# A decode block with its gradients: one kernel, the same instructions in another order

## The chip, the cores and the metric

The kernel runs on one core of one Trainium2 chip. The metric is device time in microseconds (us), from launch to end, as the median of several runs. The profile is one further execution; its span runs from the first to the last instruction on the core and leaves out what the device does before and after it.

## What is computed

The forward pass is a layer norm, a grouped attention over a cache and a gated bilinear layer, summed. The kernel returns that sum and the gradients with respect to all eight inputs that are differentiated.

```
xn = layernorm(x)                                   # x: 2 x 1 x 576
q  = (xn @ wq) -> 32 heads of 128                   # wq: 576 x 4096
p  = softmax(q . k_cache / sqrt(128))               # caches: 2 x 16 x 4096 x 128, two heads share one
A  = (p . v_cache) @ wo                             # wo: 4096 x 576
B  = ((xn @ w_gate) * (xn @ w_up)) @ w_down         # 576 x 4608, 4608 x 576
out = x + A + B
returned: out, and d(out . grad_out) / d(x, k_cache, v_cache, wq, wo, w_gate, w_up, w_down)
```

All inputs and outputs are bf16. There are only two rows of x, so nearly all the work is reading the caches and weights once and writing gradients of the same shapes once.

## The kernel before

**Tiling.** A cache head is one tile of 128 x 4096 (1 MiB), loaded by one DMA. The kernel walks 16 steps s; a step is one group of two cache heads for one of the two batch rows. Each step loads two heads of k and two of v (L1142), transposes them in 32 x 32 blocks on VectorE (DVE, L465), scores them on TensorE (PE, L1267), does the softmax in small operations on PE, DVE and ScalarE (ACT), contracts the probabilities and the score gradients with the caches (L1441), and forms the gradients of v and k as outer products (L1289). GpSimd (POOL) builds the block-diagonal operands of these outer products (L1255). Every step stores four tiles of 1 MiB: two heads of out_3 (gradient of v) and two of out_2 (gradient of k).

**Weights.** wq and wo come in eight slices, one per group (L1164, L1169); gate, up and down come in nine slices of 512 columns (L1184, L1191, L1197). Their gradients are also outer products (L726, L763, L825), stored as out_4 to out_8.

**Evictions.** An outer product is made in units. A unit fills a PSUM tile (three of them, `ps_o`) and is then copied as bf16 into a store tile, by ACT (L469) or DVE (L471). A 1 MiB store needs four units of 1024 columns. This copying and the block transposes are most of what ACT and DVE do. Below, a copy of 1024 columns is called a wide eviction.

**Order.** No engine's order is written by hand. Each piece of work is a generator (`turn`, `attend`, `dscores`, `outer`, `contract`, `fronts`, `backs`, `mlp`, `load_kv`, `load_ws` and so on). While the kernel is being built, the class `Order` (L88 to L262) runs all generators against assumed costs and decides which one goes next on each engine. Among the candidates of one engine that can start within `SLACK` of the earliest, the smallest priority goes first. A priority is `STEP * s + PR[name]`, with `HEAD` or `TAIL` added in the first two and last two steps, and a single offset from `OFF[name][s]`. An eviction goes to ACT or DVE by the earlier assumed end, with `BIAS` against DVE. `WQ_AT`, `WO_AT` and `MLP_AT` say after which cache load each weight slice is loaded. What comes out is a fixed program: one instruction list per engine, with semaphore waits.

**Queues.** All large DMAs, loads and stores alike, are issued by SyncE (SP) on one queue, 229 of them in order (here counted as row 1 to row 229). A row waits at SP for the store's evictions or for the load's free tile, and all rows behind it wait too. There are 16 tiles of 1 MiB for loads, transposes, store tiles and gate/up slices; at most 6 hold caches, 10 transposes, 5 stores and 2 gate/up slices. A DMA may be issued when the one eight before it has landed.

Of the kernel before, what the change touches and what calls it, by code (L numbers as in the profile page):

```python
# [104 lines left out]
class Order:  # L105

    HOP, TAIL, DRAIN = 0.07, 0.18, {"PE": 0.0, "ACT": 0.1, "DVE": 0.075, "POOL": 0.0}

# [86 lines left out]
    def run(self):  # L195
        while self.streams:
# [8 lines left out]
            if e is not None:  # L205
                t, _, s, e = min((c for c in cand if c[3] == e and c[0] <= t + SLACK[e]), key=lambda c: (c[1], c[0]))
            r = s.req
            value = None
            if r[0] in ("op", "any"):
                cost = r[2] if r[0] == "op" else next(c for x, c, _ in r[1] if x == e)  # L210
                quad = r[3] if len(r) > 3 else None
                if e == "PE":
                    end = t + cost + self.TAIL
                    if quad is not None and self.quad[:2] == (1 - quad, t):
                        cost, end = 0.02, max(t + self.TAIL, self.quad[2]) + 0.02
                    self.quad, self.kind = (quad, t + cost, end), r[6]
# [46 lines left out]
def EV(cols):  # L263
    return ("any", [("ACT", 0.16 + cols * 0.00083, 0.0), ("DVE", 0.145 + cols * 0.00104, cols / 1024 * BIAS)])

# [21 lines left out]
def PRIO(prio):  # L287
    return ("prio", prio)


def DMA(engine, cost, nbytes, row=8192):
# [3 lines left out]


NBIG, NWW, NBD = 16, 5, 3
CAP = {"kv": 6, "X": 10, "st": 5, "G": 2}
OFF = {"mload": {0: 271.6, 1: -102.6, 2: -55.0, 3: -1.2, 4: 302.0, 5: -37.8, 6: -3.1, 7: -261.9, 8: -10.9, 10: 33.1,
       11: 0.8, 12: -207.4, 13: 133.1, 14: -7.7, 15: 159.7}, "wload": {0: 133.7, 1: 303.1, 2: 22.2, 3: 90.3,  # L300
# [7 lines left out]
       11: 190.3, 12: -28.6, 13: -116.3, 14: -697.9, 15: 68.4}, "load": {0: 14.2, 1: -78.4, 2: 45.7, 3: 100.8,  # L308
       4: -197.6, 5: 28.3, 6: 554.3, 7: 177.4, 8: 2.5, 9: -143.0, 10: -2.3, 11: -21.3, 12: 8.4, 13: -73.3, 14: 100.6,
       15: -142.0}, "front": {0: -179.7, 1: 85.4, 2: -277.2, 3: -256.2, 4: 1826.5, 5: 49.9, 6: 24.7, 7: 68.7,  # L310
       8: 74.6, 9: -133.5, 10: 299.2, 12: -72.9, 14: -82.2}, "turn0": {0: -74.5, 1: 12.8, 2: -59.7, 4: -98.2,
       5: -13.7, 6: 27.8, 7: -195.0, 8: 25.3, 9: -324.6, 10: 62.5, 11: 150.3, 12: 36.5, 13: 374.6, 14: 6.0,
       15: 40.1}, "con": {0: -246.4, 1: 1581.7, 2: 912.6, 3: -19.4, 4: -192.0, 5: -376.3, 6: -83.8, 8: 66.8,
       9: -106.8, 10: 1369.4, 12: 147.6, 13: 65.7, 14: 198.1, 15: 79.0}, "W0": {0: 31.7, 1: -255.2, 2: 62.9,
       3: -322.1, 4: -90.7, 5: -152.2, 6: 579.2, 7: -124.9, 8: 27.6, 9: -89.0, 10: -18.9, 11: -62.1, 13: 324.8,
       14: 5.0, 15: 14.0}, "back": {0: -32.5, 1: 35.1, 2: -23.7, 3: -119.2, 4: 97.7, 5: 800.9, 6: -2327.5, 9: -276.5,
# [3 lines left out]
       9: -447.4, 10: 31.8, 11: -210.3, 12: -58.4, 13: -249.2, 14: -11.7, 15: 118.0}, "dsc": {0: -165.3, 2: -11.7,  # L320
       3: -436.2, 4: 52.6, 5: -31.9, 7: 88.0, 8: -832.8, 9: 9.9, 10: -27.9, 12: -325.8, 14: 576.3, 15: -5.7},
       "mlp": {0: 894.9, 1: 15.9, 3: -552.7, 4: -163.6, 5: -290.8, 6: 30.0, 7: -24.7, 9: -5.3, 10: -0.7, 11: -155.0,
       12: -3.1, 13: 1.8, 14: 185.9, 15: 66.1}, "att": {0: 223.1, 1: 245.8, 2: -323.8, 4: 2.7, 5: -249.3, 7: -26.2,
       8: -319.6, 9: -120.7, 10: -196.9, 11: -385.5, 12: -86.1, 13: 62.5, 14: 3.3, 15: -375.0}, "conv": {1: 35.5,
       2: 158.9, 3: 36.7, 4: 96.9, 5: -12.0, 6: 28.4, 7: 88.3, 9: 84.0, 10: 537.9, 11: -9.1, 12: -109.0, 13: 291.0,
       14: 0.9, 15: 65.7}}
MLP_AT = [1.54, 11.84, 12.88, 7.42, 26.87, 116.29, 33.85, 48.49, 96.78]
WQ_AT = [-22, 9, 14, 22, 14, 17, 46, 47]
WO_AT = [-45, -45, -9, -46, 33, 37, 23, 31]
LATENCY, DRY = {"SP": 0.5, "ACT": 0.5, "POOL": 0.57}, 0.4  # L330
LM, LAG = 0.66, 3.43
CLK = 2.0
BIAS = 0.186
SLACK = {"PE": 0.09, "ACT": 0.26, "DVE": 0.4, "POOL": 5392037994838238.0, "SP": 5703748027825.79}
STEP = 28.0
HEAD = {"turn0": -123.1, "turn1": -2289.3, "att": -2854.2, "dsc": -818.2, "con": 709.7, "out1": -2234.5,
        "out0": 965.3, "front": 1154.9, "back": -1312.3, "W0": 566.4, "W1": -1455.9, "BD1": 458.6, "BD0": 2899.0,
        "conv": -1146.6, "load": -3357.2}
TAIL = {"turn0": 905.5, "turn1": 2241.7, "att": -614.0, "dsc": -353.2, "con": 2724.6, "conv": 1530.3, "out1": 5670.9,
        "out0": -405.8, "front": -274.2, "back": 1989.7, "W1": 1283.8, "BD1": -1838.9, "BD0": -790.0, "load": 134.3,  # L340
        "W0": 1916.8}
PR = {"turn0": 854.2, "turn1": 1429.3, "att": -2428.5, "dsc": -1571.7, "conv": 280.9, "con": -1020.5, "out1": 3897.0,
      "out0": 1865.4, "front": 130.7, "back": 822.0, "W0": -2573.1, "W1": 268.5, "BD1": 2424.3, "BD0": -1416.8,
      "mlp": -908.1, "wout": -411.3, "store": -2408.5, "load": -294.1, "wload": -4334.0, "fin": -803.5,
      "const": 5061.6, "mload": -1458.5}


def pr(name, s):
    edge = {} if type(s) is not int else HEAD if s < 2 else TAIL if s > 13 else {}
    return STEP * s + PR[name] + edge.get(name, 0) + OFF.get(name, {}).get(int(s), 0)  # L350


@with_exitstack
def kernel(
# [53 lines left out]
    def tiles(tag, n, shape, dtype=BF16):  # L408
        od.ring(tag, n)
        return [const.tile(list(shape), dtype, name=f"{tag}{i}") for i in range(n)]  # L410

    kv_t = X_t = st_t = G_t = T_t = tiles("big", NBIG, [P, NCH * Dh])
    od.share("big", {**CAP, "T": 1})
    Xt_t = tiles("Xt", 1, [P, 2 * FS])
# [183 lines left out]
    def front():  # L598
# [36 lines left out]

        yield PRIO(PR["const"])
        yield WAIT(Econst)
# [133 lines left out]
    def wide_outer(rhss, dst, p, event):  # L771
        width, last = FS * len(rhss), []
        for d0 in (0, 2):
# [39 lines left out]
    def tail_outer(rhss, dsts, p, event, w0=0):  # L813
# [34 lines left out]
    def mlp(i, hh, sl, Lgu, Ld, wd_slot):  # L848
# [302 lines left out]
    def load_w(item):  # L1151
# [20 lines left out]
        else:  # L1172
# [20 lines left out]
            for hh, k in enumerate(ks):  # L1193
# [317 lines left out]
    def final_dx():  # L1511
# [80 lines left out]
```

## Time and profile before

| | us |
|---|---|
| median of 3 runs | 470.13 (469.51 to 470.38) |
| span of the profiled execution | 465.4 |
| PE busy, share of span | 372.3, 80% |
| DVE | 372.8, 80% |
| ACT | 333.6, 72% |
| POOL | 143.2, 31% |

The page is read from the DMA line down: the share of the DMA engines first, then the engines that feed the queue, then single stages of 5 us, in which busy time, granted PE clock, DMA share and GB/s stand side by side. Matmuls are pipelined, so a busy PE is not a PE at its peak.

### The profile page before, as it was taken

How to read it: one execution, taken by the hardware profiler on the slowest of the kernel's cores; microseconds unless marked ns; L12 is line 12 of the kernel's file. 1: busy time of each engine (PE TensorE's matmuls, PEld its weight loads, DVE VectorE, ACT ScalarE, POOL GpSimd, SP SyncE). 2: the span in 40 equal slices, each digit the busy share in tenths (PEclk: the TensorE clock that was granted, in tenths of full speed). 3: DMA queues.
4: the chain of work that ended last, by engine and by line, in shares of the span. 5: the costliest groups of instructions: out<-in, count | busy, mean ns of one | idle time of the engine just before them, and what ended most of it. 6: DMA issues, size and time to landing. Idle time of an engine off the chain costs nothing.

```text
span 465.4 us, 15712 instructions
## 1 busy us (share of the span) xinstructions
PE 372.3 (80%) x6750; PEld 213.0 (46%) x6750; DVE 372.8 (80%) x711; ACT 333.6 (72%) x512; POOL 143.2 (31%) x174
## 2 busy tenths in 40 slices
PE   1688779888987777888788877789788978977886
PEld 1545355546443344455555354455424533544443
DVE  8887888878779787879887778788878866877883
ACT  3268638969986687675777775678778968687874
POOL 0740042403407343470015341600743316033200
PEclk9997675877776677677775696756866665677865
DMA  8999999999999999999999999999999999999995
GB/s 316 414 410 420 411 421 387 417 416 373 371 422 422 405 424 406 420 420 421 413 407 419 419 417 404 400 350 374 418 422 424 418 411 424 423 359 390 422 368 207
DMA packets 40710, 185.97 MB, mean 400 GB/s; under 512 B 3640, under 2 KB 12352, under 8 KB 24256
## 3 DMA queue, kind: packets, MB, share of 16 engines
q1 hardware_dynamic: 40632, 184.96, 98.7%
q8 instruction: 53, 0.87, 0.7%
q14 instruction: 17, 0.14, 0.1%
q10 hardware_dynamic: 8, 0.00, 0.0%
HBM read 92.48 MB, written 92.48 MB: 397 GB/s over the span
## 4 chain that ended last, share of the span: by engine, by line
DMA 35%; PE 20%; ACT 10%; DVE 10%; issue 5%; SPq 1%; DVEq 0%; ACTq 0%
DMA out_dram<-big 20%; DMA big<-in_A_v_cache_dram 15%; ACT big L469 8%; DVE big L465 6%; PE ps_o L1289 4%; PE ps_m L1441 3%; PE ps_m L1267 3%; PE ps_o L726 2%; DVE big L471 2%; PE ps_o L763 1%; PE ps_m L677 1%; SPq L1197 1%; PE ps_m L887 1%; ACT pr L1357 0%; PE ps_o L1539 0%
## 5 line engine op out<-in xcount | busy, mean ns | idle before, releaser
L469 ACT CAST big<-ps_o 128x1024 bf16<-128x1024 f32 (+2 forms) x303 | 272.5, 957 | 51.0 <-PE ps_o L1289 31.4
L465 DVE STREAM_TRANSPOSE big<-big 128x1024 f32<-128x1024 f32 x146 | 176.3, 1223 | 21.6 <-DMA big<-in_A_v_cache_dram 10.1
L1255 POOL TENSOR_TENSOR BD<-vr,mask 128x2048 bf16<-128x2048 bf16 x32 | 115.3, 3603 | 118.6 <-PE ps_o L1289 42.9
L471 DVE CAST big<-ps_o 128x1024 bf16<-128x1024 f32 (+1 forms) x75 | 81.3, 1086 | 15.6 <-PE ps_o L1289 5.9
L1267 PE MATMUL ps_m<-big,W 128*32 128x128 bf16 x2048 | 60.2, 281 | 5.4 <-issue 3.5
L1232 POOL COPY W<-rep 32x16 bf16<-32x16 bf16 x128 | 24.5, 192 | 116.7 <-DVE rep L1006 95.8
L1267 PEld LDWEIGHTS <-W 128*32 128x32 bf16 x2048 | 47.0, 125 | 24.8 <-issue 23.7
L1289 PE MATMUL ps_o<-BD,pp 32*128 32x512 bf16 x256 | 46.1, 495 | 12.9 <-ACT big L469 7.2
L1289 PE MATMUL ps_o<-BD,dd 32*128 32x512 bf16 x256 | 43.6, 499 | 9.9 <-ACT big L469 7.8
L465 DVE STREAM_TRANSPOSE big<-ww 128x1152 f32<-128x1152 f32 (+1 forms) x25 | 33.0, 1319 | 2.4 <-DMA out_dram<-big 1.1
L1441 PE MATMUL ps_m<-big,pp 128*32 128x512 bf16 x256 | 31.9, 582 | 3.5 <-DVE pp L465 3.2
L1441 PE MATMUL ps_m<-big,dd 128*32 128x512 bf16 x256 | 28.3, 533 | 1.7 <-DVE dd L465 1.4
L1289 PEld LDWEIGHTS <-pp 32*128 32x128 bf16 x256 | 10.2, 97 | 33.2 <-issue 24.6
L1289 PEld LDWEIGHTS <-dd 32*128 32x128 bf16 x256 | 10.5, 98 | 24.8 <-issue 16.9
L1038 POOL COPY qr<-qd 128x256 bf16<-128x256 bf16 x8 | 3.2, 396 | 54.2 <-DVE qd L471 43.8
L726 PE MATMUL ps_o<-dyr,R 32*32 32x288 bf16 x256 | 18.0, 401 | 1.6 <-ACT big L469 1.5
L763 PEld LDWEIGHTS <-xnr 32*128 32x128 bf16 x368 | 12.5, 117 | 10.7 <-issue 9.2
L726 PE MATMUL ps_o<-dyr,hb 32*32 32x288 bf16 x288 | 15.5, 330 | 1.3 <-ACT big L469 1.2
L887 PE MATMUL ps_m<-big,Wdy 128*128 128x128 bf16 x162 | 15.0, 265 | 0.2
L763 PE MATMUL ps_o<-D,xnr 32*128 32x128 bf16 x256 | 13.3, 276 | 2.3 <-ACT big L469 1.7
L677 PE MATMUL ps_m<-big,wm 128*32 128x128 bf16 x416 | 13.4, 290 | 1.5 <-DVE qd L992 0.8
L1451 ACT ACTIVATE osb<-ps_m 128x512 bf16<-128x512 f32 x15 | 9.0, 597 | 7.9 <-PE ps_m L1441 7.7
(205 smaller groups left out, 483.8 us busy)
## 6 DMA issues: line engine op xcount, KB each, us to landing
out_dram<-big SPq DMA_DIRECT2D x74, 1024.0 KB, 14.0
big<-in_A_k_cache_dram SPq DMA_DIRECT2D x32, 1024.0 KB, 14.4
big<-in_A_v_cache_dram SPq DMA_DIRECT2D x32, 1024.0 KB, 12.6
out_dram<-big SPq DMA_DIRECT2D x17, 576.0 KB, 10.7
ww<-in_B_w_down_dram SPq DMA_DIRECT2D x9, 576.0 KB, 12.2
ww<-in_A_wo_dram SPq DMA_DIRECT2D x8, 576.0 KB, 7.4
ww<-in_A_wq_dram SPq DMA_DIRECT2D x8, 512.0 KB, 12.4
big<-in_B_w_gate_dram SPq DMA_DIRECT2D x4, 1024.0 KB, 14.6
```

Source lines behind the costliest of these rows:

```text
L465: nc.vector.transpose(out, in_)
L469: nc.scalar.copy(out, in_)
L471: nc.vector.tensor_copy(out=out, in_=in_)
L677: nc.tensor.matmul(dp[32 * q:32 * q + 32, 0:P], lhsT=W, rhs=view(X, 0, P, xoff(q, s), [[FS, 4], [2, 32]]), start=(s == 0), stop=(s == S - 1))
L726: nc.tensor.matmul(o[32 * q:32 * q + 32, aa, 0:HD2], lhsT=view(t, 32 * q, 32, 2 * A + aa, [[4, 32]]), rhs=dyr[32 * q:32 * q + 32, k * HD2: ...
L763: nc.tensor.matmul(o[:, aa, j * P:(j + 1) * P], lhsT=xnr[32 * a:32 * a + 32, dc * P:(dc + 1) * P], rhs=rhs(a), start=True, stop=True)
L887: nc.tensor.matmul(dh, lhsT=Wdy[:, e, 2 * k:2 * k + P], rhs=view(X[:], 0, P, 64 * k + e, [[D, FC], [2, 32]]), start=(k == 0 and e == 0), s ...
L1232: nc.gpsimd.tensor_copy(view(W_t[t][w][:], 32 * a, 32, 6 + 8 * a, [[G * WW, 4], [WW, G], [1, 2]]), view(rep_t[grp[g]["qs"]][:], 32 * a, 32 ...
L1255: nc.gpsimd.tensor_tensor(BD_t[i][:], view(vr_t[v][:], 0, P, 0, [[0, 16], [1, Dh]]), view(mask16[:], 0, P, 0, [[1, 16], [0, Dh]]), ALU.mult)
L1267: nc.tensor.matmul(sc[32 * cq:32 * cq + 32, :], lhsT=view(W[:], 0, P, (be * G + l) * WW + 6 - 4 * c2 - 2 * l, [[1, 32]]), rhs=view(X[:], 0 ...
L1289: nc.tensor.matmul(o[:, k, :], lhsT=pr2[32 * c4:32 * c4 + 32, :], rhs=BD[32 * c4:32 * c4 + 32, 8 * l + 4 * h2:8 * l + 4 * h2 + 4, :], star ...
L1441: nc.tensor.matmul(ct[32 * j:32 * j + 32, :], lhsT=view(rT, 0, P, 4 * c + 2 * l, [[1, 32]]), rhs=kv_t[kvS[s][t][l]][:, Dh * c:Dh * (c + 4) ...
```

## The change

Only constants of the planner change; no instruction is added or removed. `PR` and all entries of `OFF` are new, `HEAD` and `TAIL` are new and now also hold `mlp`, `wload` and `mload`; `BIAS` goes from 0.186 to 0.188 and the `SLACK` of PE from 0.09 to 0.06, of ACT from 0.26 to 0.25. The caps are the same. In the lists that come out (buffer numbers aside), DVE's is the same up to its instruction 434 of 711, ACT's but for one place up to its middle, and SP's in kind up to row 69. 255 wide evictions stand on ACT (247 before) and 47 on DVE (55 before).

```
-CAP = {"kv": 6, "X": 10, "st": 5, "G": 2}
-OFF = {"mload": {0: 271.6, 1: -102.6, 2: -55.0, 3: -1.2, 4: 302.0, 5: -37.8, 6: -3.1, 7: -261.9, 8: -10.9, 10: 33.1,
...
+CAP = {"G": 2, "X": 10, "kv": 6, "st": 5}
+OFF = {"turn0": {0: -1015.2, 1: -14.6, 2: -608.5, 3: -352.4, 4: -44.2, 5: -609.4, 6: 1026.5, 7: -575.3, 8: -336.9,
...
-MLP_AT = [1.54, 11.84, 12.88, 7.42, 26.87, 116.29, 33.85, 48.49, 96.78]
-WQ_AT = [-22, 9, 14, 22, 14, 17, 46, 47]
-WO_AT = [-45, -45, -9, -46, 33, 37, 23, 31]
+MLP_AT = [1.14, 5.4, 2.05, 2.45, 26.26, 69.69, 14.36, 0.0, 155.88]
+WQ_AT = [-126, 9, 14, 22, -10, -36, 47, 13]
+WO_AT = [-81, -88, -157, -95, 31, 1, -2, -56]
...
-BIAS = 0.186
-SLACK = {"PE": 0.09, "ACT": 0.26, "DVE": 0.4, "POOL": 5392037994838238.0, "SP": 5703748027825.79}
+BIAS = 0.188
+SLACK = {"PE": 0.06, "ACT": 0.25, "DVE": 0.4, "POOL": 10000.0, "SP": 10000.0}
...
-      "mlp": -908.1, "wout": -411.3, "store": -2408.5, "load": -294.1, "wload": -4334.0, "fin": -803.5,
-      "const": 5061.6, "mload": -1458.5}
+      "mlp": -735.6, "wout": -435.6, "store": -3305.7, "load": -1982.4, "wload": -3953.8, "fin": 5877.7,
+      "const": 11595.3, "mload": -2275.6}
```

The SP lists where they differ most, before and after (k and v are loads; every out is a store; 1 MiB unless said):

```
row   before                         after
60    load k (step 5)                load k (step 5), into another tile
154   store out_2                    store out_2
155   store out_8, 576 KiB           stores of out_6, out_7 tails
...
202   store out_4 tail               store out_4 tail
203   load v (step 15)               store out_4, 768 KiB
204   load v (step 15)               load v (step 15)
205   load gate                      load v (step 15)
206   store out_4, 768 KiB           load gate
207   load up                        load up
208   load down                      store out_4, 768 KiB
209   store out_4, 768 KiB           load down (last load)
210   stores up to row 229           stores up to row 229
```

More of the change, by code (lines that the diff above doesn't have):

```diff
@@ L297 @@
 NBIG, NWW, NBD = 16, 5, 3
-CAP = {"kv": 6, "X": 10, "st": 5, "G": 2}
-OFF = {"mload": {0: 271.6, 1: -102.6, 2: -55.0, 3: -1.2, 4: 302.0, 5: -37.8, 6: -3.1, 7: -261.9, 8: -10.9, 10: 33.1,
-       11: 0.8, 12: -207.4, 13: 133.1, 14: -7.7, 15: 159.7}, "wload": {0: 133.7, 1: 303.1, 2: 22.2, 3: 90.3,
[7 rows of a table removed]
[L308 to L316, printed above, removed]
[3 rows of a table removed]
[L320 to L326, printed above, removed]
@@ L327 @@
-MLP_AT = [1.54, 11.84, 12.88, 7.42, 26.87, 116.29, 33.85, 48.49, 96.78]
-WQ_AT = [-22, 9, 14, 22, 14, 17, 46, 47]
-WO_AT = [-45, -45, -9, -46, 33, 37, 23, 31]
+CAP = {"G": 2, "X": 10, "kv": 6, "st": 5}
+OFF = {"turn0": {0: -1015.2, 1: -14.6, 2: -608.5, 3: -352.4, 4: -44.2, 5: -609.4, 6: 1026.5, 7: -575.3, 8: -336.9,
+       9: -48.1, 10: 73.1, 12: 183.6, 13: 1140.9, 15: 354.0}, "turn1": {0: -158.8, 1: 373.8, 2: -399.3, 3: -123.5,
+       4: -561.8, 5: 1792.7, 6: 184.6, 7: -225.4, 8: -1188.5, 9: -525.0, 10: -1211.4, 11: -134.5, 12: 1399.2, 13:
+       -786.3, 14: 125.3, 15: -889.4}, "att": {0: -320.6, 1: 25.1, 2: -524.3, 3: 1437.6, 4: -1231.0, 5: 704.1, 6:
+       -946.7, 7: -1656.2, 8: -1046.6, 9: 659.5, 10: -617.2, 11: -169.8, 12: 46.5, 13: -31.6, 14: -222.6, 15:
+       1033.5}, "dsc": {0: -1811.3, 1: -9.9, 2: 131.1, 3: 301.3, 4: -3.2, 5: 235.2, 6: -975.3, 8: 26.8, 9: 229.2,
+       10: -420.4, 11: 210.0, 12: 19.1, 13: 299.2, 14: 9.4}, "conv": {0: -2015.6, 1: 231.3, 2: -0.4, 3: -50.3, 4:
+       -1165.8, 5: 1061.5, 6: 135.8, 7: 373.5, 8: -2359.6, 9: 3.5, 10: 1574.4, 11: 172.6, 12: 216.0, 13: 448.3, 14:
+       255.6, 15: 10.6}, "con": {0: -32.2, 1: 1152.5, 2: 1696.5, 3: 720.8, 4: 638.1, 5: 104.8, 6: -260.9, 7: -158.3,
[3 rows of a table added]
+       9: -103.2, 10: -395.3, 11: 2850.9, 12: 125.0, 13: 2376.4, 15: -25.5}, "front": {0: -90.0, 1: 2844.9, 2:
+       -805.5, 3: -966.7, 4: 1527.3, 5: 109.2, 6: 51.9, 7: -924.3, 8: -171.1, 9: -1466.9, 10: -796.2, 11: 95.0, 12:
+       407.0, 13: 194.7, 14: 42.9, 15: -116.8}, "back": {0: -1180.5, 1: 591.1, 2: -2708.2, 3: 979.9, 4: 556.1, 5:
[7 rows of a table added]
+       13: -595.2, 14: -250.1, 15: 5.1}, "mlp": {0: 248.5, 1: 1168.1, 2: -620.3, 3: -398.1, 4: -321.8, 5: 2002.0, 6:
+       162.1, 7: -3.7, 8: -33.1, 9: -2.4, 10: 1014.3, 11: 985.4, 12: 835.4, 13: -9.7, 14: 314.7, 15: -413.5},
+       "load": {0: 1074.9, 1: -427.7, 2: 2940.0, 4: -302.0, 5: 501.3, 6: 157.2, 7: 2723.0, 8: 41.7, 9: 175.7, 10:
+       -1207.2, 11: -514.7, 12: -5.8, 13: 248.9, 14: 607.8, 15: -253.7}, "wload": {0: -271.1, 1: 208.8, 2: -1828.2,
+       3: 108.3, 4: 438.0, 5: -390.0, 6: 623.3, 7: 89.8, 8: -357.2, 9: -50.4, 10: 1806.6, 11: 48.4, 12: -1247.3, 13:
+       3030.4, 14: 857.3, 15: 1037.7}, "mload": {0: 867.2, 1: -358.1, 2: -1319.2, 3: 100.2, 5: 58.5, 6: -3446.8, 9:
+       -71.5, 10: -371.1, 11: -312.3, 12: 9.2, 13: 247.9, 14: 253.2, 15: -7.2}}
@@ L332 @@
 CLK = 2.0
-BIAS = 0.186
-SLACK = {"PE": 0.09, "ACT": 0.26, "DVE": 0.4, "POOL": 5392037994838238.0, "SP": 5703748027825.79}
+BIAS = 0.188
+SLACK = {"PE": 0.06, "ACT": 0.25, "DVE": 0.4, "POOL": 10000.0, "SP": 10000.0}
 STEP = 28.0
[L336 to L343, printed above, removed]
-      "mlp": -908.1, "wout": -411.3, "store": -2408.5, "load": -294.1, "wload": -4334.0, "fin": -803.5,
-      "const": 5061.6, "mload": -1458.5}
+HEAD = {"turn0": -995.0, "turn1": -3790.2, "att": -3348.0, "dsc": 396.0, "conv": -832.5, "con": 1401.5, "out1":
+        -1892.2, "out0": 2828.7, "front": 21.6, "back": 291.8, "W0": -1455.9, "W1": -155.0, "BD1": 1364.6, "BD0":
+        2903.1, "mlp": 2389.4, "load": -3080.4, "wload": 394.7, "mload": -742.1}
+TAIL = {"turn0": 3370.1, "turn1": 9221.8, "att": 665.4, "dsc": 359.0, "conv": 2694.5, "con": 2347.7, "out1": 7925.6,
+        "out0": -1730.3, "front": 756.2, "back": 2986.8, "W0": 3398.4, "W1": -331.2, "BD1": -2581.8, "BD0": -508.7,
+        "mlp": -5065.9, "load": 6824.2, "wload": 208.6, "mload": 3569.7}
+PR = {"turn0": 1475.9, "turn1": 1614.7, "att": -4652.5, "dsc": -2890.4, "conv": 226.3, "con": -1413.1, "out1":
+      3893.4, "out0": 2308.0, "front": 679.0, "back": 881.2, "W0": -1279.8, "W1": -624.6, "BD1": 2069.1, "BD0":
+      -1551.4, "mlp": -735.6, "wout": -435.6, "store": -3305.7, "load": -1982.4, "wload": -3953.8, "fin": 5877.7,
+      "const": 11595.3, "mload": -2275.6}
 def pr(name, s):
```

20 rows, old and new, of the table OFF are left out of this document.

## The prediction

> **What bounds the kernel now.** I read the DMA lines of the page first, then the cost of single instructions, then stages. Each slice line holds 40 equal parts of the span.
>
> ```profile
> span 465.4 us, 15712 instructions
> DMA  8999999999999999999999999999999999999995
> GB/s 316 414 410 420 411 421 387 417 416 373 371 422 422 405 424 406 420 420 421 413 407 419 419 417 404 400 350 374 418 422 424 418 411 424 423 359 390 422 368 207
> q1 hardware_dynamic: 40632, 184.96, 98.7%
> ```
>
> One queue moves 184.96 MB and fills the 16 DMA engines for 98.7% of the span. The bytes and the sizes of the transfers don't change, so an order can win only where that queue runs short: the slices near 371, near 350 and 359, and the end. The same places by stage; the columns are PE, PEld, DVE, ACT and POOL busy time, then granted PE clock, DMA share and GB/s.
>
> ```profile
> 105.00:130.00 25.00, 21.70 (x490) 12.84 (x482) 20.35 (x36) 24.30 (x34) 8.74 (x10) 0.77 0.98 376
> 305.00:325.00 20.00, 18.19 (x393) 11.63 (x397) 18.50 (x29) 16.56 (x23) 0.00 (x0) 0.54 0.95 354
> 370.00:375.00 5.00, 4.95 (x92) 2.31 (x91) 2.58 (x9) 3.02 (x7) 0.00 (x0) 0.66 1.02 422
> 410.00:425.00 15.00, 10.13 (x158) 4.63 (x144) 13.67 (x23) 11.61 (x19) 7.06 (x2) 0.79 0.99 354
> 425.00:465.40 40.40, 32.35 (x539) 18.22 (x537) 27.35 (x52) 27.49 (x39) 3.75 (x2) 0.67 0.86 346
> ```
>
> A full stage shows a share of 1.02 (370 to 375). The shortfall, as time, is (1.02 - share) / 1.02 x length: 1.0 us at 105 to 130, 1.4 us at 305 to 325, 0.4 us at 410 to 425, and 6.3 us in the last 40.4 us. So 9.1 us are all that any order could win there. The mean rates are lower than the shares because short rows move fewer bytes in the same DMA time; no order changes that.
>
> In the last stage DVE and ACT are busy for only 27 of 40 us each: it is a chain of small steps and evictions between PE, ACT and DVE, with the stores waiting. The waits of SP around the gap at 305 say what the queue wants there:
>
> ```profile
> SPq L695 <- ACT big L469: 8.3, 3, 4.8
> SPq L695 <- DVE big L471: 1.7, 1, 1.7
> ```
>
> These are stores (L695) waiting for evictions, 8.3 us for ACT's and 1.7 us for DVE's. Evictions and transposes cost:
>
> ```profile
> L469 ACT CAST big<-ps_o 128x1024 bf16<-128x1024 f32 x247 | 238.0, 1022 | 37.2 <-PE ps_o L1289 31.4 <-PE ps_o L763 1.9 <-DMA out_dram<-big 1.9
> L471 DVE CAST big<-ps_o 128x1024 bf16<-128x1024 f32 x55 | 66.3, 1209 | 9.4 <-PE ps_o L1289 5.9 <-PE ps_o L763 1.8 <-issue 1.6
> L471 DVE CAST big<-ps_o 128x576 bf16<-128x576 f32 x20 | 14.9, 747 | 6.3 <-PE ps_o L726 4.8 <-ACT big L469 1.3 <-issue 0.2
> L469 ACT CAST big<-ps_o 128x576 bf16<-128x576 f32 x48 | 29.5, 644 | 12.6 <-PE ps_o L726 12.1
> ```
>
> **The change, part by part.** The lists of the two programs can be laid side by side, and where I speak of work ahead of a row I add the mean durations of the groups, such as these, over the instructions that ACT or DVE must finish before SP may issue it.
>
> *The first 60%.* DVE's list is the same up to 434 of 711, and the work ahead of SP's rows is the same up to row 138 except at rows 25 to 27 against 36 to 38, where the stores of two MLP blocks change places, at row 60, and at 70 to 74 and 104 to 106, where loads and stores pass each other by one place. All lie in stages with a full queue (a store that had to wait there would cost its wait, at most the 1.0 us found at 105 to 130), except row 60: there the load goes to another tile that comes free 20 us of DVE work earlier. Row 61 behind it still waits for the same ACT evictions, so of the 1.0 us at 105 to 130 I take 0.2 (0 to 1.0).
>
> *Wide evictions that change engine.* 47 instead of 55 on DVE, 255 instead of 247 on ACT: 8 x 1.209 = 9.7 us less on DVE, 8 x 1.022 = 8.2 us more on ACT. While the queue is full this costs and gives nothing; what covers it is the queue. Without that cover ACT would be late by up to 8.2 us at the very end, where DVE would be early by 9.7 us. I count it only in the stages below.
>
> *The gap at 305.* At rows 154 to 158 the new lists ask 5 to 15 us less of DVE and 1 to 4 us less of ACT ahead of the same kind of store, except 3 us more of DVE for the 576 KiB store. ACT was what the stores waited for, so a lead of 1 to 4 us can close a gap of 1.4 us. I take 0.9 (0 to 1.4); what is late next is row 159, a store in place of a v load.
>
> *New order at rows 139 to 200.* Loads and stores pass each other by up to four places, two out_2 stores move back by 13 and 29 rows, and three out_3 stores move forward by 11, 11 and 23. Bytes stay as they were. A new gap is possible; the trace has no row for one, so I bound it by the largest it shows in mid-kernel, 1.4 us, and by none, since these stages are full today. I take +0.4, nearer to none.
>
> *The last loads.* In the new list a 768 KiB store stands at row 203, ahead of the last two v loads, the gate, up and down loads: all of them wait behind it.
>
> ```profile
> 408.89 0.98 SPq L1142 DMA_DIRECT2D big<-in_A_v_cache_dram  x2
> 410.57 1.22 SPq L695 DMA_DIRECT2D out_dram<-big  x1
> 419.53 1.25 DVE L465 STREAM_TRANSPOSE big<-big 128x1024 f32<-128x1024 f32 x1 [0.74 <-DMA big<-in_A_v_cache_dram]
> ```
>
> Before, the v loads went out at 408.89 and the store at 410.57, when its evictions were done; the store's bytes, 0.79 MB at 422 GB/s, are 1.9 us of queue. DVE did wait for the landing at 419.53, but for 0.74 us only, so part of a later landing hides behind other transposes. Price between 0 and 1.9; I take +1.0.
>
> *The work left for the end.* The last softmax step's exponent marks the point in both lists from which the end runs.
>
> ```profile
> 424.39 0.40 ACT L1349 ACTIVATE ex<-ex,negb 128x128 f32<-128x128 f32 x1
> ```
>
> Behind it, before: DVE has 11 wide evictions and 2 of 576 columns, ACT 21 and 6. After: 7 and 3, and 21 and 5. So 4 x 1.209 - 0.747 + 0.644 = 4.7 us of evictions are done earlier instead. Shared by two engines that is 2.4 us. If the end shrank in proportion to their busy time (54.8 us in the stage from 425), it would be 40.4 x 4.7 / 54.8 = 3.5 us; if the chain of small steps alone sets it, 0. I take 2.3, since stores wait for both engines' evictions right up to the end. The queue allows it: the stage moves 346 GB/s x 40.4 us = 14.0 MB, which at 422 takes 33 us.
>
> *Sum.* -0.2 - 0.9 + 0.4 + 1.0 - 2.3 = -2.0 us. The span of the profiled execution goes from 465.4 to 463.4. The median of the runs, 470.13, lies 4.7 above that span; kept as it is, this gives 468.1 us. Single bounds added up run from -5.9 to +3.3, which is 464.2 to 473.4.
>
> One rule speaks against any gain. The Trainium skill, "DMA: Bandwidth & Descriptors", section Specifications, gives about 358 GB/s as one core's limit at HBM; 184.96 MB would then take 517 us, and no order would matter. The rows above move 422 GB/s over whole slices, so this trace does not agree, and I give the rule no weight.
>
> **The rivals.**
>
> *The end starves (slower).* The store at row 203 needs 5 us more of ACT's list than the v load that stood there. If it holds the queue until its evictions are done, the five loads behind it land 1.9 us later or more, and if the last step's chain, not the number of evictions, sets the end, nothing comes back: 470.1 + 1.9, with the one new gap of up to 1.4, is 472.0 to 473.4. For it: DVE waits for that landing today. Against it: a v load lands 12.6 us after its issue in the median, most of it spent behind earlier rows, so a late issue need not show.
>
> ```profile
> big<-in_A_v_cache_dram SPq DMA_DIRECT2D x32, 1024.0 KB, 12.6
> ```
>
> It decides once SP's pause before row 203 is longer than the queue's backlog.
>
> *The gaps only move (no change).* The queue is 98.7% full, the gap at 305 goes elsewhere, and the later loads eat the shorter end: 470.1. For it: the terms are small and of both signs. Against it: the work for the end really is less.
>
> *All gaps close.* 1.0 + 1.4 + 0.4 + 3.5 = 6.3 us less: 463.8. Against it: the order has not changed much where the first gap lies.
>
> *The PE clock.* In two stages close together the clock is 1.00 and then 0.50, though PE is as busy or busier:
>
> ```profile
> 90.00:95.00 5.00, 3.00 (x123) 2.06 (x120) 2.71 (x7) 3.52 (x6) 0.00 (x0) 1.00 1.03 406
> 100.00:105.00 5.00, 5.00 (x45) 2.11 (x42) 3.47 (x7) 3.53 (x5) 0.00 (x0) 0.50 1.02 418
> ```
>
> Another order may meet more of the slow clock at the end. The end stage has 0.67 on average and 32.35 us of PE work; at 0.60 that work would be 32.35 x 0.67 / 0.60 = 36.1 us, 3.8 longer, and with half of it on the path the time is 470.1 - 2.0 + 1.9 = 470.0, with all of it and the loads' 1.9, 473.8. The Trainium skill, "TensorE: Matmul & The Clock Gate", Part 1, says that the clock halves after an idle window of about 3.4 us and that work releases it; these two rows show the reverse, so I don't forecast the clock from how busy PE is.
>
> **How the numbers follow.** My forecast (a shorter end, fewer gaps) 0.54, within 465.8 to 469.2; the end starves 0.17; gaps only move 0.15; all gaps close 0.06; the clock 0.08. A measurement of this kernel tells apart about 0.2%, or 0.9 us. Faster by more: forecast and all gaps closed, 0.60. Within: 0.15. Slower: 0.25, from the starved end and the clock. Point 468.1; the range 465.0 to 473.6 leaves out half of the closed gaps and the worst of the two slow cases.
>
> **What would show it.** Right: the DMA share at the stage near 305 to 325 rises to 1.00 or more; the last exponent lies within 2 us of 424.39 and the end comes at most 39 us behind it; stages up to 100 us look as before. Wrong: SP pauses more than 3 us before row 203 and the share falls below 0.95 behind it; a new slice under 380 GB/s between 320 and 405; or the last exponent later than 427, which would mean that the steps before it lost what the end won.

## The result, and the profile after

| | before | after |
|---|---|---|
| median of 6 runs each, us | 470.25 (469.40 to 471.70) | 466.26 (464.97 to 467.36) |
| ratio to before, 95% interval | | 0.9915 (0.9896 to 0.9934) |
| span of the profiled execution, us | 465.4 | 464.1 |

The changed kernel is 4.0 us faster; 2.0 us were forecast, with 468.1 as the time and 465.0 to 473.6 as the range. The two profiled spans differ by only 1.3 us, so something about the first profile has to be explained too. The page of the changed kernel, the lines read first:

```profile
span 464.1 us, 15709 instructions
DMA  8999999999999999999999999999999999999994
GB/s 312 416 409 422 410 426 395 408 414 372 355 415 422 407 422 407 411 423 425 414 405 418 419 423 420 424 414 411 400 406 395 394 422 424 424 404 349 422 384 186
q1 hardware_dynamic: 40632, 184.96, 98.7%
```

The dip of before in slices 27 and 28 (350, 374) is gone (414, 411). The dip at slice 11 is deeper (355 for 371), and slices 29 to 32, at 394 to 406, lie lower than before's 418 to 424. The same by stage; the columns are busy time of PE, PEld, DVE, ACT and POOL, then granted PE clock, DMA share and GB/s:

```profile
105.00:130.00 25.00, 23.66 (x450) 12.84 (x435) 17.88 (x33) 22.25 (x30) 8.74 (x10) 0.50 0.96 367
250.00:305.00 55.00, 45.69 (x901) 28.23 (x890) 43.47 (x82) 42.49 (x63) 17.46 (x22) 0.75 1.02 421
305.00:325.00 20.00, 16.11 (x288) 8.41 (x283) 14.47 (x23) 13.32 (x18) 3.37 (x1) 0.50 1.02 412
325.00:405.00 80.00, 69.14 (x1068) 35.78 (x1068) 62.46 (x114) 64.40 (x105) 31.92 (x41) 0.65 1.01 409
415.00:420.00 5.00, 4.17 (x89) 2.10 (x85) 2.52 (x3) 4.65 (x7) 1.37 (x1) 0.78 0.82 307
425.00:445.00 20.00, 18.54 (x308) 9.50 (x301) 16.49 (x29) 18.93 (x28) 1.31 (x1) 0.76 1.01 422
425.00:464.10 39.10, 32.41 (x530) 18.20 (x523) 24.21 (x50) 27.32 (x40) 1.31 (x1) 0.63 0.85 341
```

The same stages of the first profile of before, where the prediction didn't show them:

```profile
250.00:305.00 55.00, 43.78 (x823) 25.46 (x822) 41.18 (x74) 36.91 (x60) 19.85 (x22) 0.72 1.01 411
325.00:405.00 80.00, 67.04 (x985) 32.88 (x984) 62.28 (x112) 63.35 (x96) 31.97 (x41) 0.66 1.02 420
...
425.00:445.00 20.00, 17.06 (x307) 9.88 (x305) 16.19 (x28) 16.80 (x25) 3.75 (x2) 0.81 1.02 425
```

Three things are to be seen. At 305 to 325 the share went from 0.95 to 1.02 and the rate from 354 to 412 GB/s: the gap is closed. In the 55 us up to 305, ACT does 5.6 us and DVE 2.3 us more work than before, and both do less in the next 20 us: work was pulled forward. And between 325 and 405 the rate fell from 420 to 409 GB/s under a full share.

The last exponent in the changed kernel (first and last start are the two numbers behind "us"):

```profile
L1350 ACT ACTIVATE ex<-ex,negb x16: 376/400/413, 20.8 to 425.1; 128x128 f32<-128x128 f32 x16
```

It starts at 425.1 instead of 424.39, and the end comes 39.0 us behind it instead of 41.0. From the exponent to the end, the DMA view of before has

```profile
DMA packets 3825, 14.22 MB, mean 347 GB/s; under 512 B 316, under 2 KB 2085, under 8 KB 2539
```

and that of the changed kernel

```profile
DMA packets 3553, 13.28 MB, mean 340 GB/s; under 512 B 296, under 2 KB 2028, under 8 KB 2311
```

so 0.94 MB less is left there, 2.2 us at 422 GB/s. SP at the store that the prediction worried about, row 203 at 405.59, and at the other 768 KiB store, row 208 at 414.01 (start, duration, engine and line, what is issued):

```profile
402.79 0.47 SPq L696 DMA_DIRECT2D out_dram<-tl  x1
405.59 0.39 SPq L696 DMA_DIRECT2D out_dram<-big  x1
406.13 1.58 SPq L1143 DMA_DIRECT2D big<-in_A_v_cache_dram  x2
...
414.01 5.05 SPq L696 DMA_DIRECT2D out_dram<-big  x1
419.11 0.80 SPq L1198 DMA_DIRECT2D ww<-in_B_w_down_dram  x1
```

SP paused 2.3 us (403.26 to 405.59) ahead of row 203, below the 3 us named as a wrong sign. It stood 5 us at row 208, and at 415 to 420 the share fell to 0.82 (0.90 in the second profile of the changed kernel).

**Bytes moved by a given time.** Since one queue carries everything, I count what it had moved at three places. Each fence has three windows of one profile: from 0 to 325 us, from 0 to 405 us, and from 445 us to the end. First the first profile of before, then the second one (the run `base_again` below, span 467.7), then the changed kernel, then its second profile (`change_again`, span 465.1).

```profile
DMA packets 28963, 131.12 MB, mean 403 GB/s; under 512 B 2596, under 2 KB 7848, under 8 KB 17778
DMA packets 34637, 164.70 MB, mean 407 GB/s; under 512 B 3168, under 2 KB 9060, under 8 KB 19940
DMA packets 2461, 5.47 MB, mean 268 GB/s; under 512 B 177, under 2 KB 1909, under 8 KB 2147
```

```profile
DMA packets 28747, 130.23 MB, mean 401 GB/s; under 512 B 2586, under 2 KB 7838, under 8 KB 17574
DMA packets 34507, 163.76 MB, mean 404 GB/s; under 512 B 3153, under 2 KB 9045, under 8 KB 19925
DMA packets 2601, 6.42 MB, mean 283 GB/s; under 512 B 193, under 2 KB 1925, under 8 KB 2181
```

```profile
DMA packets 29358, 132.57 MB, mean 408 GB/s; under 512 B 2633, under 2 KB 7877, under 8 KB 18180
DMA packets 34718, 165.30 MB, mean 408 GB/s; under 512 B 3176, under 2 KB 9068, under 8 KB 19948
DMA packets 2358, 4.89 MB, mean 256 GB/s; under 512 B 168, under 2 KB 1898, under 8 KB 2085
```

```profile
DMA packets 29254, 132.27 MB, mean 407 GB/s; under 512 B 2620, under 2 KB 7833, under 8 KB 18076
DMA packets 34653, 164.82 MB, mean 407 GB/s; under 512 B 3170, under 2 KB 9062, under 8 KB 19942
DMA packets 2435, 5.27 MB, mean 262 GB/s; under 512 B 173, under 2 KB 1905, under 8 KB 2148
```

The counts of packets under 2 KB at 405 us agree within 23, and behind 445 within 27, so there the megabytes can be compared. At 325 us the counts under 8 KB differ by 402 and 502, so that place is less sure. Taking the first profiles together and the second ones together, at the 422 GB/s of a full stage:

| | first pair | second pair |
|---|---|---|
| more moved by 325 us | 1.45 MB, 3.4 us | 2.04 MB, 4.8 us |
| more moved by 405 us | 0.60 MB, 1.4 us | 1.06 MB, 2.5 us |
| less left at 445 us | 0.58 MB, 1.4 us | 1.15 MB, 2.7 us |
| difference of the spans | 1.3 us | 2.6 us |

So the whole difference of the spans is there at 405 us: won between 250 and 325 (at 250 the changed kernel had moved 0.28 and 0.50 MB less), partly given back between 325 and 405, and then carried to the end without gain or loss. The last stretch itself didn't get better: behind 445 before needs 20.4 us for 5.47 MB, that is 13.0 us at 422 GB/s and 7.4 us on top; its second profile 7.5 on top, the changed kernel 7.5 and 7.6.

More bytes by a given time doesn't have to mean less idle time. The queue's share of the whole span is 98.7% in both first profiles and 98.6% in both second ones: the share that was missing at 305 to 325 is now missing elsewhere, as at 415 to 420, and the span is shorter by as much as the same 40,632 packets took less time in sum. The packet records of the traces say where. A packet of 8 KiB took 329 and 333 ns on average between 250 and 325 us in the two profiles of before and 312 in both of the changed kernel; between 325 and 405 it took 313 in both of before and 321 and 323 in the changed kernel. In the first pair the 16 engines were busy for 1.4 us more between 250 and 325, in the second for 2.2; the rest of what was won there came with the shorter packets. Why they are shorter isn't shown.

### The profile page after: what moved, and what is told of

The parts are those of the page before. It is cut to its first block, busy times and chain, and to the rows that moved or that the text cites. A ratio compares the mean times of both kernels' runs of the same rounds, so it can differ in the third digit from the quotient of the medians.

```text
span 464.1 us, 15709 instructions
## 1 busy us (share of the span) xinstructions
PE 372.6 (80%) x6750; PEld 213.9 (46%) x6750; DVE 366.2 (79%) x708; ACT 337.7 (73%) x515; POOL 143.1 (31%) x174
## 3 DMA queue, kind: packets, MB, share of 16 engines
q1 hardware_dynamic: 40632, 184.96, 98.7%
## 5 line engine op out<-in xcount | busy, mean ns | idle before, releaser
L470 ACT CAST big<-ps_o 128x1024 bf16<-128x1024 f32 (+2 forms) x309 | 278.9, 963 | 50.6 <-PE ps_o L1290 23.8
L472 DVE CAST big<-ps_o 128x1024 bf16<-128x1024 f32 (+1 forms) x69 | 73.4, 1065 | 17.8 <-PE ps_o L764 7.7
L1268 PE MATMUL ps_m<-big,W 128*32 128x128 bf16 x2048 | 57.3, 272 | 4.3 <-issue 1.8
L1268 PEld LDWEIGHTS <-W 128*32 128x32 bf16 x2048 | 45.5, 121 | 23.5 <-issue 22.5
L1290 PE MATMUL ps_o<-BD,dd 32*128 32x512 bf16 x256 | 45.8, 523 | 9.2 <-ACT big L470 5.6
L1290 PE MATMUL ps_o<-BD,pp 32*128 32x512 bf16 x256 | 44.5, 465 | 9.1 <-ACT big L470 7.5
L1442 PE MATMUL ps_m<-big,dd 128*32 128x512 bf16 x256 | 30.7, 578 | 1.6 <-DVE dd L466 0.9
L1442 PE MATMUL ps_m<-big,pp 128*32 128x512 bf16 x256 | 29.2, 545 | 3.5 <-DVE pp L466 2.8
L764 PEld LDWEIGHTS <-xnr 32*128 32x128 bf16 x368 | 13.6, 119 | 14.3 <-issue 13.3
L764 PE MATMUL ps_o<-D,xnr 32*128 32x128 bf16 x256 | 14.7, 285 | 4.9 <-ACT big L470 3.6
L888 PEld LDWEIGHTS <-Wdy 128*128 128x128 bf16 x162 | 14.4, 127 | 3.0 <-issue 2.7
```

The costliest lines, as they stand in the source:

```text
L470: nc.scalar.copy(out, in_)
L472: nc.vector.tensor_copy(out=out, in_=in_)
L764: nc.tensor.matmul(o[:, aa, j * P:(j + 1) * P], lhsT=xnr[32 * a:32 * a + 32, dc * P:(dc + 1) * P], rhs=rhs(a), start=True, stop=True)
L888: nc.tensor.matmul(dh, lhsT=Wdy[:, e, 2 * k:2 * k + P], rhs=view(X[:], 0, P, 64 * k + e, [[D, FC], [2, 32]]), start=(k == 0 and e == 0), s ...
L1268: nc.tensor.matmul(sc[32 * cq:32 * cq + 32, :], lhsT=view(W[:], 0, P, (be * G + l) * WW + 6 - 4 * c2 - 2 * l, [[1, 32]]), rhs=view(X[:], 0 ...
L1290: nc.tensor.matmul(o[:, k, :], lhsT=pr2[32 * c4:32 * c4 + 32, :], rhs=BD[32 * c4:32 * c4 + 32, 8 * l + 4 * h2:8 * l + 4 * h2 + 4, :], star ...
```

## The experiments

All times are medians; ratios are to the kernel before, run on the same chip, with 95% intervals.

| kernel | us | ratio |
|---|---|---|
| base_again (before, unchanged) | 470.12 (468.51 to 471.68) | 1.0005 (0.9989 to 1.0020) |
| change_again (after, unchanged) | 466.47 (465.84 to 468.24) | 0.9926 (0.9905 to 0.9948) |
| late_only | 466.62 | 0.9923 (0.9908 to 0.9938) |
| middle_only | 475.05 | 1.0106 (1.0089 to 1.0124) |
| end_only | 468.39 | 0.9974 (0.9963 to 0.9986) |
| more_bytes | 469.23 | 0.9985 (0.9973 to 0.9998) |
| more_evictions | 469.34 | 0.9993 (0.9971 to 1.0015) |
| v_first | 466.45 | 0.9937 (0.9922 to 0.9952) |
| down_first | 466.40 | 0.9935 (0.9921 to 0.9948) |
| loads_first | 465.71 | 0.9926 (0.9911 to 0.9940) |
| gap_closed | 469.48 | 1.0000 (0.9986 to 1.0013) |
| fewer_left | 469.10 | 0.9994 (0.9983 to 1.0005) |

**Both kernels again.** No edit.

> The kernel before, unchanged, to see what its usual execution looks like: six executions of the changed kernel had 1.8 us between span and time, while the profile of before has a span 4.7 us below the median of its runs. If that profile was an unusually quick execution, the spans here lie near 468.5 and the extra 3 us stand in some stage of the new profile (the gap at 305 to 325, or the end). If the gap between span and time differs by kernel, spans lie near 465.4 with times near 470.

> The changed kernel once more, for a second profile beside one of before from the same chip. Span 463 to 466, time 1.8 us above it. The DMA share at 305 to 325 is 1.00 or more again if that gap was closed by the order and not by chance; the end stands 39 us behind the last exponent again.

The 12 executions of base_again had a median span of 467.9 us, the changed kernel's first six 464.45. The time was 1.8 us above the span in the profiled executions of both (469.51 against 467.7, 465.85 against 464.1). So the first profile of before, at 465.4, was a quick execution: 2.5 us below the usual span, and below all 81 spans of this kernel recorded beside the experiments, whose lowest is 466.0. What it lacked stands in its second profile:

```profile
250.00:305.00 55.00, 43.86 (x831) 25.14 (x830) 41.64 (x76) 36.99 (x60) 21.43 (x22) 0.69 1.01 403
305.00:325.00 20.00, 18.21 (x401) 12.09 (x395) 17.34 (x27) 16.11 (x23) 0.00 (x0) 0.50 0.93 334
```

403 and 334 GB/s where the first profile had 411 and 354: the gap has no fixed size in the kernel before, and the profile behind the prediction showed a small one. The changed kernel's second profile has there:

```profile
305.00:325.00 20.00, 15.16 (x317) 8.77 (x311) 14.67 (x24) 13.86 (x20) 3.60 (x1) 0.67 1.02 414
```

**Parts of the order.** For these kernels the planner holds both sets of constants and changes from one to the other when its own clock passes SWITCH; every instruction stays. late_only has before's constants, then the new ones from 250; end_only the same from 345; middle_only the new ones, then before's from 345; fewer_left the new ones, then before's from 395.

```
+SWITCH = 250.0
...
-                    cand.append((t, s.prio, s, e))
+                    cand.append((t, self.rank(s), s, e))
+            if self.phase == 0 and cand and min(c[0] for c in cand) >= SWITCH:
+                self.phase = PHASE[0] = 1
+                continue
```

> The priorities of before rule while the first 250 us of the planner's clock are laid out, those of after from there on: SP's rows up to 138 are those of before (row 60's load in the old tile, row 70 a load, rows 105 and 106 in the old order), all engines' lists behind it are those of after. If the gain lies in the late part, ratio 0.990 to 0.993 against before, as the full change has. If the early rows carry part of it (the load of row 60 that needs 20 us less of DVE's list), 0.995 to 0.998.

The whole gain is there with before's order in the first half: what the change does up to SP row 138 is worth nothing that can be measured.

> The lists of after up to about row 180 of SP (345 us on the planner's clock), then the priorities of before rule. The stores at rows 154 to 158 need as little as after asks; behind the last exponent 34 wide evictions are left (before 32, after 28), and the last v loads stand ahead of the 768 KiB store as before. If the gap at 305 to 325 is the main gain, ratio 0.994 to 0.997. If the work left for the end is the main gain, the end is 40 us or more behind the last exponent and the ratio is 0.998 to 1.003.

Slower than either, though the gap is closed (1.02 and 415 GB/s at 305 to 325) and 132.21 MB were moved by 325 us, nearly as in the changed kernel. By 405 only 163.65 MB were. Two stages of it:

```profile
325.00:405.00 80.00, 67.27 (x1031) 34.96 (x1027) 62.33 (x113) 58.73 (x95) 31.98 (x41) 0.65 1.00 393
425.00:445.00 20.00, 17.49 (x329) 10.20 (x328) 15.42 (x29) 14.80 (x23) 7.20 (x2) 0.70 0.83 326
```

ACT does 5.7 us less between 325 and 405 than in the changed kernel and the queue moves 393 GB/s. That work is then missing at the end, where the share falls to 0.83 and SP's longest waits are stores' for evictions (6.3 us for one of DVE, 5.6 for one of ACT). A closed gap is worth nothing if the evictions behind it fall back.

> The lists of the kernel before up to SP row 179, so the gap at 305 to 325 stays (DMA share .93 to .95); behind it the planner goes on with the new constants, which leaves 27 wide evictions behind the last exponent instead of 32, with the last v loads ahead of the 768 KiB store. Theory A (the prediction's: closed gap and shorter end are two gains, and the end goes with the evictions left): the end shrinks from 41.0 to 38 to 39 us though the gap stays, time 467 to 468. Theory B (one account: what the queue doesn't move in the gap it moves at the end, and the end is as long as the bytes left at the last exponent take): with the gap left open 14.0 MB or more are still left behind the exponent, or the exponent comes later; time 469.3 to 471.

The gap stayed and still 1.7 us were won, between the two expectations:

```profile
305.00:325.00 20.00, 18.18 (x407) 12.03 (x403) 18.39 (x29) 16.41 (x24) 0.00 (x0) 0.52 0.95 352
410.00:425.00 15.00, 13.86 (x252) 7.11 (x245) 12.48 (x23) 12.70 (x16) 3.60 (x1) 0.57 1.01 380
```

Its last exponent came at 427.6 and the end 38.3 us later. So neither theory holds as it stood: part of a late gain can be had without the gap. Where it was won isn't shown. The rate of 380 GB/s at 410 to 425, where the two profiles of before have 354 and 353, points there. But this profile had moved 139.09 MB by 345 us, when SP's list was still that of before, and the two profiles of before 139.47 and 138.54, and behind 445 it left 5.45 MB against 5.47 and 6.42: all of it lies within what before shows from one execution to the next.

> The changed kernel up to SP row 210 with the order of the last evictions of before's constants: 23 wide evictions behind the last exponent instead of 28, 50.5 us of listed ACT and DVE work there instead of 55.6. The five are done shortly ahead of the exponent. If work left sets the end alone (0.44 us of end per us of work in the runs so far): end 36.8 instead of 39.0 and time 464.3 to 465. If evictions done just ahead of the exponent hold it up as long: the exponent 1.5 to 2.5 us later, time 466 to 467.

Five wide evictions fewer behind the exponent than in the changed kernel, and 2.6 us slower. By 405 us it had moved 165.36 MB, as the changed kernel did. The exponent came at 426.7, the end 40.5 us later, and the queue ran short in between:

```profile
425.00:445.00 20.00, 18.38 (x316) 11.00 (x317) 15.80 (x28) 14.36 (x23) 2.89 (x1) 0.67 0.97 389
```

The share is 0.97 against 1.01. (The rate, 389 against 422 GB/s, can't be compared: short rows stand earlier here, and behind 445 us 806 packets under 2 KB are left instead of 1,898.) Behind the exponent one eviction of DVE held SP for 9.5 us; in the changed kernel no eviction did for more than 3.3. So the number of evictions left is no measure of the end by itself; it matters whether each store's evictions are ready when its row comes up.

**Bytes and evictions added.** Both are edits of the changed kernel.

```
+    stores, EXTRA = [], 45
+    spare = nc.dram_tensor("spare", (P, 4096), BF16, kind="Internal").ap()
...
             nc.sync.dma_start(d, x)
+            if nbytes == 1 << 20:
+                stores.append(x)
+                if len(stores) == EXTRA:
+                    nc.sync.dma_start(spare, x)
```

> The changed kernel with one more 1 MiB store on SP's queue behind row 154 (about 302 us), of the same tile into a scratch tensor in DRAM; nothing else differs on any engine. It takes the queue 1.05 MB / 422 GB/s = 2.5 us, as a gap of that size would. Theory A: all that follows moves 2.5 us, the last exponent from 425 to 427.6, the end stays 39.0 us long; time 469. Theory B: the exponent stays within 1 us of 425 to 426, about 14.3 MB instead of 13.3 are left behind it and the end is 41 to 41.5 us long; time 468.7 to 469.2. A rival, that this part of the kernel has slack and the end is a chain of its own: time up by less than 1, to 467.4 at most.

2.8 us more than the changed kernel, for 2.5 us of queue. The exponent moved from 425.1 to 427.7 and the end stayed 38.9 us long, which is theory A's place for it: the exponent waits for the last loads on the same queue and moves with them. Queue time taken at 300 us is paid in full at the end.

```
         nc.scalar.activation(c["ex"][:], c["ex"][:], AF.Exp, bias=c["negb"][:], scale=SCALE, accum_out=c["z"][:])
+        if s == NS - 1:
+            twice.update(ACT=2, DVE=2)
...
         ev(e, o_t[i])
+        if cols == 1024 and twice[e]:
+            twice[e] -= 1
+            ev(e, o_t[i])
```

> The changed kernel with four wide evictions done twice behind the last exponent, the first two of ACT and the first two of DVE there (2 x 1.03 + 2 x 1.22 = 4.5 us of work); the bytes are the same. Theory A: the end goes with the evictions left, half of 4.5 us or more: time up by 2.2 to 3.3, 468.7 to 469.8. Theory B: the end goes with the bytes left, the evictions hide behind the queue: up by 0 to 0.8, 466.5 to 467.3, with the DMA share up to 445 us still above 1.00.

4.5 us of evictions more, 2.9 us slower: the gain is gone, though the queue had moved 165.17 MB by 405 us, as in the changed kernel. The queue ran short where it had been full:

```profile
425.00:445.00 20.00, 17.04 (x246) 8.79 (x248) 14.81 (x25) 16.03 (x24) 2.02 (x1) 0.67 0.94 391
```

With the work put back, ACT and DVE have some 60 us of it behind the exponent (each instruction at its group's mean duration), about as much as before. But before has 14.22 MB to move meanwhile and this kernel 13.3, and before's queue stayed full over this stage (425 GB/s). So it seems to be the smaller amount of work at the end that keeps the bytes moved earlier from being lost again; the doubled evictions all stand at the first places behind the exponent, though, where before's additional ones needn't. Whether less work is a gain of its own, the next runs show.

**The last loads.** In the changed kernel, one or two stores are held back by a few rows; nothing else differs. The lines are those of v_first; down_first has {208: 209}, loads_first both.

```
+    rows, HOLD = [], {203: 205}
+    def sync(dst, src):
+        rows.append((dst, src))
+        if len(rows) in HOLD:
+            return
+        nc.sync.dma_start(dst, src)
+        for k, n in HOLD.items():
+            if n == len(rows):
+                nc.sync.dma_start(*rows[k - 1])
```

> The changed kernel with the 768 KiB store of row 203 issued behind the two v loads of rows 204 and 205; nothing else differs. If the store ahead of the loads costs what the prediction took, 1.0 us (0 to 1.9), the wait of DVE for v at 420 us shrinks from 2.6 to below 1.0 us and the time falls to 465.5 (464.6 to 466.5). Theory B: the queue moves the same bytes, DVE's wait shrinks but the hole in the DMA share at 415 to 420 (0.82) stays, since SP stands at row 208 there; time 466 to 466.6.

> The changed kernel with the second 768 KiB store (row 208) issued behind the last down load (row 209); nothing else differs. SP stands 5 us at that store while the share falls to 0.82 at 415 to 420 (1.0 us lost). If that hole is on the path: share there 0.95 or more, time 465.4 to 466.0. If the end takes it up, as it did with the other store moved: 466.3 to 466.8 with a longer end behind an earlier exponent.

> The changed kernel with both 768 KiB stores moved: row 203 behind the two v loads, row 208 behind the down load. If either order of the last loads costs anything: 464.9 to 465.9. If the chain behind the last exponent with its evictions sets the end whatever the order of the last rows: 466.2 to 466.9.

v_first did what was expected of the wait (DVE's for v fell from 2.6 to 0.6 us, and the hole in the share at 415 to 420 was filled) and won nothing:

```profile
415.00:420.00 5.00, 5.00 (x76) 1.95 (x79) 4.37 (x4) 4.29 (x6) 2.13 (x1) 0.50 0.99 378
```

Its exponent came at 424.6 and the end 40.3 us behind it. down_first left the hole as it was (0.77), and SP then stood 5.1 us at the down load, which speaks against the store at row 208 as its cause. loads_first, with both stores moved, says the most. Its exponent, and the DMA view from there to the end at 463.9:

```profile
L1361 ACT ACTIVATE ex<-ex,negb x16: 376/402/413, 21.4 to 423.2; 128x128 f32<-128x128 f32 x16
```

```profile
DMA packets 3790, 14.11 MB, mean 347 GB/s; under 512 B 311, under 2 KB 2076, under 8 KB 2504
```

The lists of ACT and DVE are those of the changed kernel, with the same 28 wide evictions behind the exponent, and yet the end is 40.7 us long with 14.11 MB to move: as in before (41.0 us, 14.22 MB), not as in the changed kernel (39.0 us, 13.28 MB). What moved is the exponent, from 424.39 and 426.7 in the two profiles of before to 423.2. So the end goes with the bytes left, as long as the evictions keep up. All profiles here fit that: in the eleven with a share of 1.01 or more at 425 to 445, 12.8 to 14.2 MB were left at the exponent and the end took 38.4 to 41.0 us, about 2.1 us more for each MB; in the other three, middle_only, more_evictions and fewer_left, it took longer for the bytes left. The changed kernel's end is shorter than that of loads_first because two stores stand ahead of its last loads: their bytes are moved before the exponent, and the exponent waits for them. The gain itself lies earlier.

loads_first has the lowest median of all, 465.71 against 466.47, but its ratio is that of the unchanged kernel; whether it is better can't be told from these runs.

**The gap alone.** In the kernel before, four units (matmuls and wide evictions) are left out shortly ahead of row 158, so parts of out_2, out_3 and out_6 aren't written with their values.

```
+    units, LEAVE = [], (178, 179, 180, 183)
...
+        left_out = cols == 1024 and len(units) in LEAVE
+        if not left_out:
+            mms(o_t[i])
...
+        if not left_out:
+            ev(e, o_t[i])
```

> The kernel before, with four units left out (matmuls and wide evictions, two on ACT and two on DVE) shortly ahead of the store of row 158, so parts of out_2, out_3 and out_6 aren't written with their values; all rows and bytes of the queue stay. If the gap at 305 to 325 is worth its size (1.4 us in the first profile of before, 1.8 in the second), the DMA share there rises to 1.00 or more, the end behind the last exponent stays 41 us and the time falls by 1.4 to 2.0, to 468.1 to 468.7. If the change's gain there comes from other work than the gap (order, evictions), the time falls by less than 0.8. More than 2.5 would mean that ACT and DVE, not the queue, set the middle of the kernel.

The gap didn't close and the time didn't move:

```profile
305.00:325.00 20.00, 17.72 (x383) 11.61 (x376) 16.75 (x26) 16.38 (x23) 0.00 (x0) 0.50 0.92 341
```

So this run can't price the gap. It does show that the gap isn't a matter of 2 us of evictions on each engine. What SP's stores waited for on ACT between 304 and 318 us, in the second profile of before, in this run and in the changed kernel (us in total, times, longest):

```profile
SPq L695 <- ACT big L469: 9.7, 3, 5.6
SPq L697 <- ACT big L471: 11.6, 3, 8.8
SPq L696 <- ACT big L470: 2.4, 1, 2.4
```

With fewer evictions to make, ACT's came no earlier. The chain of waits in this run, in order of time:

```profile
292.78 13.37 DMA out_dram<-big
...
307.35 0.40 DVE tl L473
...
307.79 0.62 PE ps_o L770 x8
...
308.43 1.94 ACT big L471 x2
```

Here the late evictions hang on a store's landing (a tile comes free) and on PE's outer products. PE is busy for 17.7 to 18.2 of the 20 us from 305 to 325 in the four profiles with before's order there, at a granted clock of 0.50 to 0.54, and for 15.2 and 16.1 us in those of the changed kernel. That PE's share of the work is what the new order spreads out fits these rows, but no run changed it alone.

## Why the prediction was right in sign and short in size

- **The base: a quick execution.** "The median of the runs, 470.13, lies 4.7 above that span; kept as it is." Where time and span of one execution are known they are mostly 1.8 to 2.0 us apart; the rest of the 4.7 was the quick execution that the profile had caught. The distance itself drops out of a forecast of a change. What it cost is that the gaps were sized from an execution in which they were small. Median spans went from 467.9 to 464.45, so the change was worth about 3.5 us of span, where the sum said 2.0.
- **The gap at 305: right that it closes, mis-sized, for a reason that fell.** Taken as 0.9 with 1.4 at most, from (1.02 - share) in a quick execution. By 325 us the queue had gained 3.4 and 4.8 us. The stage ahead, 250 to 305, was counted as full at 1.01, yet moved 403 to 411 GB/s and now 421. So the premise failed that an order can win only where the share is short ("9.1 us are all that any order could win there", and of the mean rates, "no order changes that"): much of what was won came with shorter packets. "ACT was what the stores waited for, so a lead of 1 to 4 us can close a gap" is half right: SP's waits for ACT did shrink with the gap, from 8.3 and 9.7 to 2.4 us, but leaving 2 us of evictions out on both engines closed nothing, so ACT's own list alone didn't make them late.
- **The new order at rows 139 to 200: right sign, too small.** +0.4 was taken, with 1.4 as the largest gap seen. Between 325 and 405 the changed kernel gave back 0.85 and 0.98 MB, 2.0 and 2.3 us, without a gap: the share stayed at 1.01 and the rate fell. A bound made from shares couldn't see that.
- **Row 60: nothing.** -0.2 was taken. The share at 105 to 130 was 0.96 and 0.97 after, 0.98 and 1.01 before, and late_only has the full gain without that row.
- **The last loads: +1.0 taken, nothing measured by moving either store, 0.7 at most by moving both.** The store at row 203 held up no issue; only its bytes went ahead, so DVE waited 2.6 us for v instead of 0.7, which cost nothing in time. In the chain of waits of the changed kernel, PE frees the tile of the v load behind it after the store has gone out:

```profile
405.95 0.17 PE ps_m L684 x11
406.11 0.02 issue
406.13 13.87 DMA big<-in_A_v_cache_dram
```

- **The work left for the end: the number came as forecast, its meaning didn't.** "At most 39 us behind it" was said, and it is 39.0. But with the same evictions left and the loads first, loads_first has 40.7. The stretch is shorter for the 0.94 MB that are moved ahead of the exponent, 2.2 us of queue, and they were won earlier: behind 445 us both kernels need 7.4 to 7.6 us beyond their bytes. Gap and end were added as two gains and are one, seen at two places. The price of the work, 0.49 us per us, was not far off for adding it (2.9 for 4.5) and taking it away won nothing in fewer_left, whose order differs too.
- **The rivals.** The starved end didn't come, but middle_only and more_evictions show that it was near. Gaps moved only in part. The PE clock was lower at the end, 0.63 for 0.67, with no loss to be seen in the stretch behind 445.

That the sum came within 2 us was in part luck, since its errors had both signs: a gain counted twice, a loss of 1.0 that isn't there, a gap and a give-back both too small. What is shown is when the bytes were won and that the late part of the order wins them; what in that order does it, PE's work or another wait, stays open.

## What to carry to other kernels

Where one queue is the bound, ask by which time how many bytes have been moved, and compare at times when the mix of packet sizes agrees: that shows where a gain arises and where it is given back, which shares near 1.00 and distances between landmarks don't. Before a span is used as a base, set it against the runs' own spans, since a single profile can lie 2.5 us off and show its gaps too small. Work that a full queue hides can have a price on one side only: adding 4.5 us of it cost 2.9, while an order with 5.1 us less of it, changed in other ways too, won nothing.

## What was not expected of the hardware

A full DMA share isn't a fixed rate. Between 325 and 405 us the kernel before moved 420 GB/s in 5,674 packets and the changed kernel 409 GB/s in 5,360, with shares of 1.02 and 1.01. The mix differs: 2,162 packets under 8 KB against 1,768. But packets of the same 8 KiB also took longer, 313 and 321 ns on average. It wasn't a lack of work for the queue: in the stages of 5 us between 340 and 370 us of the changed kernel's first profile, with averages up to 358 ns, three rows or more were issued and not yet landed throughout. Nothing in the runs says why.

The same program's gap varied between executions: 0.95 and 354 GB/s at 305 to 325 in one profile of before, 0.93 and 334 in the next, while the two profiles of the changed kernel agree within 2 GB/s.
